# Attention, two gated layers: a longer written order, other denominators, other column groups in PV

## The chip, the cores and the metric

The kernel runs on one core of a Trainium2 chip. The metric is the device time of one execution in microseconds; the kernel before took 491.09 us (median of 3 runs, 490.27 to 493.12). Names used below: PE is TensorE, the matrix engine; DVE is VectorE; ACT is ScalarE; POOL is GpSimd; SP is SyncE, whose queue issues the transfers.

## The reference, cut to what matters

```
# mLSTM: 2 batches x 8 heads, 768 positions, 40 per head
m_new = max(f + m, i);  f_s = exp(f + m - m_new);  i_s = exp(i - m_new)
C = f_s * C + i_s * outer(v, k);   n = f_s * n + i_s * k
denom = max(|n . q|, 1);           y = sigmoid(o_gate) * (C q) / denom
# layer 1 on 1536 rows of 320, inner width 1536
x = (sigmoid(x @ w_gate) * (x @ w_val)) @ w_out
# layer 2: the same widths, rows normalised first, silu gate
xn = x / rms(x) * g;  x = (silu(xn @ w_gate) * (xn @ w_val)) @ w_out
```

## The kernel before

**Tiles and stages.** The 768 positions are cut into 6 chunks of 128 (c) and the 2 batches (b). For each chunk and batch the attention is computed in four quarters (q, four heads each): a scan turns the gates into weights between positions (F), S is k against q, P the product of the two, PV the product of P with v, I the part that comes from the state C, U and UC the new state. H then adds PV and I, multiplies by the output gate and divides by the denominator. The result x is transposed on PE (XP, L492 and L493) and split into a high and a low float32r part (XH, XL). Layer 1 takes chunks 0 to 3 one by one and 4 and 5 as a pair (name p), layer 2 takes the chunks in three pairs, the first called q. Each layer has 12 tiles of weights (f, 0 to b in hexadecimal): T is the up-projection (eight matmuls with the gate half, eight with the value half: L549 for one chunk, L596 for a pair), S and M the activation and the products, H the split, Y the down-projection (L577, L574, L627).

**Weights.** A packed weight tile is loaded (LW, LZ; line 179), its top half is unpacked into one of two scratch tiles `tops` (WT, ZT; L192 on ACT, L194 on DVE), DVE combines it with the mantissa (WM, WO, ZM; L199), and ACT, DVE and POOL split it further. Layer 2's raw tiles and the low half of layer 2's transposed input share one tag, `wraw`, with two buffers; `new_xT2` takes the high and the low half's buffers together.

**PV.** From chunk PB = 2 on, P and v are split into three bf16 parts each, and a head takes three accumulating matmuls of 126, 84 and 42 columns into three column groups (L416), which H adds in three additions a quarter (L226). Chunks 0 and 1 use float32 directly (L418).

**Denominators.** `abs_1` makes max(|nq|, 1) with two DVE instructions (L441, L442), a reciprocal follows (L461, L475), and a product with x broadcast over the head (L226; three of chunk 0's four quarters on POOL).

**What sets the order.** PLAN is a written list of step names; the steps are issued in that order and pinned, so each engine and SP's queue execute their shares in it. It goes up to layer 2's steps q0 and q1 (NP = 2), after which the remaining steps of layer 2 are issued in a loop and placed by the scheduler. PE opens with 13 idle matmuls (WARM, L869), and six steps D (`m_idle`, L555) issue two idle matmuls each.

Of the kernel before, what the change touches and what calls it, by code (L numbers as in the profile page):

```python
# [7 lines left out]
F32 = mybir.dt.float32  # L8
F32R = mybir.dt.float32r
# [28 lines left out]
PB = 2  # L38
# [3 lines left out]
N32 = (4,2)  # L42
# [7 lines left out]
K00 H01b WO0 WM0 F02 PV00 H00a Lqk01 S01 WG0 F03 P03 Lgr D0 Lmr Ltok01 Rf1 Ri1 LW1 LW2 Rf2 WLG0 H00b V01 WLH0 WOH0 XR00 Rie Rfe U00 Rer P02 K02 Rz PV03  # L50
D1 PV02 K03 Lfd Lqg10 Lsel Lqk10 Lf10 O01 WR0 WLR0 WLS0 U01 WT1 XP00 H03a WM1 Lf11 H02a WO1 H03b UC00 Ltok10 Lqg11 LW3 H02b Rt1 D2 Rt2 WT2 UC01 Lf13
LW4 Lqk11 Lf12 XR01 WR1 WO2 WM2 XP01 D3 WLR1 XH00 XL00 D4 D5 XH01 XL01 Rel UM00 WR2 Rc1 F11 Rg F10 WG2 WG1 Rgc Rc2 T00 S10 WLG1 WLS1 TS00 WOH2 WLS2
WLH1 TH00 P10 P11 Y000 Y001 I10 WT3 K11 V10 T01 PV11 PV10 IH10 WLR2 WO3 WM3 WLG2 K10 WG3 WLH3 WLG3 TS01 WR3 TH01 WT4 T02 TS02 H10a WLS3 Ltok11 WLR3 F12
F13 S11 Y011 TH02 P13 P12 UM01 V11 T03 I11 Y010 PV13 Y021 PV12 WO4 WM4 TS03 O10 H10b WR4 O11 WG4 LW6 LW9 Lqk20 LW5 Ltok20 WLR4 H10c IH11 U10 WLS4 WLH4
# [960 lines left out]
```

## Time and profile before

| | |
|---|---|
| median of 3 runs | 491.09 us |
| the profiled execution | 491.04 us |
| its span, first to last instruction | 489.3 us |
| PE busy | 472.6 us (97%) |
| DVE busy | 277.6 us (57%) |
| ACT busy | 208.6 us (43%) |
| POOL busy | 207.2 us (42%) |
| mean granted clock of PE | 0.978 |

Times in the trace count from the first instruction. Matmuls overlap, so the difference between starts says more of their rate than the mean of one, and a float32 matmul is recorded as two. The granted clock is 1.00 at 2.4 GHz and half of that at 1.2 GHz.

### The profile page before, as it was taken

Reading aid. Unit: us, or ns where it says so; the run is one execution under the profiler, and the core shown is the slowest. Engines: PE = TensorE matmul, PEld = TensorE weight load, DVE = VectorE, ACT = ScalarE, POOL = GpSimd, SP = SyncE. Lnnn points to the kernel's source line nnn. Section 1 sums busy time; section 2 is a strip of 40 time slices with the busy share of each in tenths; the row PEclk is TensorE's granted clock in tenths of the full one; section 3 lists DMA queues with packets and bytes.
Section 4 is the critical chain, followed back from the end, with each engine's and each line's share of the span. In section 5 each row is a group of like instructions: output and inputs, shape, how many; then the busy total and the mean of one; then the engine's idle time right before and its main releaser. Section 6 shows DMA issues by size and latency. Waiting matters only on the chain.

```text
span 489.3 us, 8000 instructions
## 1 busy us (share of the span) xinstructions
PE 472.6 (97%) x3074; PEld 421.7 (86%) x3074; DVE 277.6 (57%) x518; ACT 208.6 (43%) x459; POOL 207.2 (42%) x252
## 2 busy tenths in 40 slices
PE   8999999998999999999999997999999999999997
PEld 5888899998998999978888886888888888888886
DVE  6789668896799998947366655222342222332223
ACT  4655686544534435632657654222332222322222
POOL 3555577556575546222466763322222221323221
PEclk9589999999999999999999998999999999999999
DMA  6699901143051431334433220000010000100001
GB/s 220 244 333 380 373 32 58 43 140 101 15 141 58 144 110 57 125 107 161 162 109 132 82 81 1 0 1 0 1 54 1 1 1 0 55 0 1 1 1 54
DMA packets 13277, 43.80 MB, mean 90 GB/s; under 512 B 1623, under 2 KB 5095, under 8 KB 13239
## 3 DMA queue, kind: packets, MB, share of 16 engines
q1 hardware_dynamic: 13094, 43.16, 26.1%
q8 instruction: 24, 0.39, 0.3%
q10 hardware_dynamic: 144, 0.14, 0.1%
q14 instruction: 15, 0.11, 0.1%
HBM read 41.24 MB, written 2.05 MB: 88 GB/s over the span
## 4 chain that ended last, share of the span: by engine, by line
PE 71%; DVE 17%; DMA 4%; ACT 3%; issue 2%; POOL 1%; SPq 1%; ACTq 0%; DVEq 0%; POOLq 0%
PE g L596 18%; PE a L596 18%; PE o L627 17%; PE g L549 8%; PE o L577 4%; DVE hs L226 3%; DVE ft L229 3%; DMA early<-fd 2%; DVE x L226 2%; DVE p L226 1%; DMA fb<-fd 1%; DVE sig L226 1%; PE o L869 1%; PE o L549 1%; DVE p L130 1%
## 5 line engine op out<-in xcount | busy, mean ns | idle before, releaser
L130 POOL TENSOR_TENSOR ft<-p,fb 128x512 fp32r<-128x512 f32 x47 | 61.4, 1307 | 164.0 <-ACT fb L232 156.7
L549 PE MATMUL g<-xT,w 128*128 128x256 f32 x640 | 82.6, 283 | 0.4 <-DVE sig L226 0.4
L226 DVE TENSOR_TENSOR p<-p,g 128x512 f32<-128x512 f32 x36 | 24.8, 688 | 101.8 <-ACT p L600 101.8
L549 PEld LDWEIGHTS g<-xT,w 128*128 128x128 f32 x640 | 78.0, 188 | 1.4 <-DVE sig L226 0.7
L627 PE MATMUL o<-w,fb 128*128 128x320 f32 x384 | 73.5, 310 | 0.0
L596 PE MATMUL g<-xT,w 128*128 128x512 f32 x240 | 67.8, 398 | 3.6 <-DVE p L226 3.6
L627 PEld LDWEIGHTS o<-w,fb 128*128 128x128 f32 x384 | 62.2, 188 | 4.2
L596 PE MATMUL a<-xT,w 128*128 128x512 f32 x240 | 64.7, 398 | 0.0
L232 ACT ACTIVATE fb<-p 128x512 fp32r<-128x512 f32 (+1 forms) x49 | 30.4, 622 | 77.1 <-DVE p L226 58.4
L600 ACT ACTIVATE p<-g 128x512 f32<-128x512 f32 x48 | 28.5, 595 | 74.1 <-PE g L596 69.5
L226 DVE TENSOR_TENSOR p<-p,a 128x512 f32<-128x512 f32 (+1 forms) x49 | 33.0, 675 | 39.4 <-PE a L596 24.3
L596 PEld LDWEIGHTS g<-xT,w 128*128 128x128 f32 x240 | 43.4, 189 | 11.5 <-DVE p L226 4.1
L596 PEld LDWEIGHTS a<-xT,w 128*128 128x128 f32 x240 | 44.9, 190 | 9.3
L130 POOL TENSOR_TENSOR h<-sig,h 128x256 fp32r<-128x256 f32 x42 | 35.1, 838 | 39.4 <-ACT h L232 37.6
L577 PE MATMUL o<-w,h 128*128 128x320 f32 x252 | 46.5, 319 | 0.0
L627 PE MATMUL o<-w,ft 128*128 128x320 f32 x192 | 45.8, 310 | 0.0
L577 PEld LDWEIGHTS o<-w,h 128*128 128x128 f32 x252 | 37.8, 189 | 1.1
L627 PEld LDWEIGHTS o<-w,ft 128*128 128x128 f32 x192 | 32.7, 188 | 0.4
L130 POOL TENSOR_TENSOR w<-wc,w 128x256 fp32r<-128x256 f32 (+2 forms) x37 | 24.9, 677 | 18.8 <-ACT w L232 9.7
L596 PE MATMUL g<-wraw,w 128*128 128x512 f32 x108 | 31.6, 400 | 0.0
L596 PE MATMUL a<-wraw,w 128*128 128x512 f32 x108 | 31.1, 393 | 0.0
L232 ACT ACTIVATE h<-sig 128x256 fp32r<-128x256 f32 x42 | 17.3, 414 | 25.3 <-DVE sig L226 15.5
(168 smaller groups left out, 747.6 us busy)
## 6 DMA issues: line engine op xcount, KB each, us to landing
wraw<-in_w_dram SPq DMA_DIRECT2D x24, 959.8 KB, 9.0
tok<-in_tok_dram SPq DMA_DIRECT2D x10, 488.0 KB
fb<-fd SPq DMA_DIRECT2D x18, 256.0 KB, 3.3
raw<-in_qk_dram SPq DMA_DIRECT2D x24, 160.0 KB
out_dram<-xn SPq DMA_DIRECT2D x12, 160.0 KB, 1.8
qg<-in_qg_dram SPq DMA_DIRECT2D x8, 180.0 KB, 4.9
early<-in_tok_dram SPq DMA_DIRECT2D x2, 488.0 KB
early<-fd SPq DMA_DIRECT2D x2, 256.0 KB
```

The costliest lines, as they stand in the source:

```text
L130: eng.tensor_tensor(out=out, in0=a, in1=b, op=ALU.subtract)
L226: eng.tensor_tensor(out=out, in0=a, in1=b, op=op)
L229: v.tensor_tensor_scan(out=out, data0=a, data1=b, initial=initial, op0=op0, op1=op1)
L232: a_.activation(out=out, in_=x, func=AF.Copy, scale=scale)
L549: nc.tensor.matmul(out=g[:, m, :], lhsT=w[:, m, ws, :], rhs=x[xs // 3][:, xs % 3, :], start=(i == 0), stop=(i == 7))
L577: nc.tensor.matmul(out=o, lhsT=h[:, hs, b * L:(b + 1) * L], rhs=wo_t[f][:, ws, :], start=(n == 1 and i == 0), stop=(n == NF and i == 2))
L596: nc.tensor.matmul(out=g, lhsT=w[:, m, ws, :], rhs=x[xs // 3][:, xs % 3, :], start=(i == 0), stop=(i == 7))
L600: a_.activation(out=s, in_=keep["w", k, f, 0], func=AF.Sigmoid)
L627: nc.tensor.matmul(out=o_ps[key][:, 0:DM], lhsT=h[hs][:, n], rhs=wo_t[f][:, ws, :], start=(c == 1 and i == 0), stop=(c == NF and i == 2))
L869: nc.tensor.matmul(out=t, lhsT=warm[:, 0:128], rhs=warm, start=True, stop=True)
```

## The change

The program's numbers change: PB from 2 to 3, NP from 2 to 5, ND from 6 to 24, and PLAN is written anew in full. Of the code, `abs_1` goes: the absolute value is an activation on ACT, the reciprocal a step of its own (H..r), and the minimum with 1 is taken in the last product, which is on DVE throughout. From chunk 3 on a head of PV takes four matmuls into two column groups (84, 42, 84, 42 columns), and H adds two groups a quarter; chunk 2 uses float32 PV. `tops` are handed out from a list of free ones. `new_xT2` takes the low half's buffer when the low half is written. Each D issues one idle matmul.

```diff
-PB = 2
+PB = 3
-NP = 2
+NP = 5
-ND = 6
+ND = 24
 PLAN = """
-Lga Gm Gf1 Gf2 Gfe Gid Gmz Gse Gi1 Gms Lgs Ltok00 Gfh Gie Gt Gfl Fb01 Fb00 Rm Lqk00 S00 F01 P01 LW0 Fb02 O00 Gtg V00 Fb03 Lms PV01 F00 H01a K01 P00 WT0
+D0 D1 D2 Lga Gm Lsel D3 D4 D5 D6 D7 D8 Gse Gms Gid Lgr Lgs Lqg10 Gf1 Lqk01 Lqk00 Rm Gf2 Gfe Gi1 Gmz Gfh Gfl Lms Fb01 Ltok01 Lmr Ltok00 Gie Gt D9 D10
...
-        up = tops[turn["t"] % 2]
-        turn["t"] += 1
+        up = free.pop(0)
...
+        left[f] = left.get(f, WC) - (n.stop - n.start)
+        if left[f] == 0:
+            left.pop(f)
+            free.append(up)
...
-                for k in range(3):
-                    n = (3 - k) * E
-                    nc.tensor.matmul(out=ps[:, 3 * i * E:3 * i * E + n], lhsT=p[:, k, i, :], rhs=w[:, 0:n], start=(k == 0), stop=(k == 2))
+                for n, (k, s0, ns, d) in enumerate(((0, 0, 2, 0), (0, 2, 1, 1), (1, 0, 2, 0), (2, 0, 1, 0))):
+                    at = (2 * i + d) * E
+                    nc.tensor.matmul(out=ps[:, at:at + ns * E], lhsT=p[:, k, i, :], rhs=w[:, s0 * E:(s0 + ns) * E], start=(n == 0), stop=(n == 3))
...
-    def abs_1(r, nq):
-        v.tensor_scalar(out=r, in0=nq, scalar1=1.0, scalar2=None, op0=ALU.max)
-        v.scalar_tensor_tensor(out=r, in0=nq, scalar=-1.0, in1=r, op0=ALU.mult, op1=ALU.max)
+    def h_abs(key, nq):
+        r = out_t[key] = p2.tile([128, 8, 1], F32, tag="r", name="r")[:, 0:nq.shape[1]]
+        a_.activation(out=r, in_=nq, func=AF.Abs)
+    def h_r(key):
+        v.reciprocal(out=out_t[key], in_=out_t[key])
+    def h_mul(eng, key, x):
+        r = out_t.pop(key)
+        eng.scalar_tensor_tensor(out=x, in0=r.to_broadcast([128, r.shape[1], D]), scalar=1.0, in1=x, op0=ALU.min, op1=ALU.mult)
...
-                pv = pv_t.pop((c, 2 * b + q))[:, 0:12 * E].rearrange("p (h s e) -> p h s e", h=4, s=3)
-                for k in range(3):
+                pv = pv_t.pop((c, 2 * b + q))[:, 0:8 * E].rearrange("p (h s e) -> p h s e", h=4, s=2)
+                for k in range(2):
                     tt(v, hs[:, 4 * q:4 * q + 4], pv[:, :, k], hs[:, 4 * q:4 * q + 4], ALU.add)
...
-    def new_xT2(pair):
-        if (2, pair) not in xT:
+    def new_xT2(pair, part):
+        t = xT.setdefault((2, pair), [])
+        if part == len(t):
...
-        for _ in range(2):
-            nc.tensor.matmul(out=g, lhsT=warm[:, 0:128], rhs=warm, start=True, stop=True)
+        nc.tensor.matmul(out=g, lhsT=warm[:, 0:128], rhs=warm, start=True, stop=True)
```

On DVE, around layer 2's first steps, before: the raw tile of weight 9 (`raw_3688`) and the two products (`p_3679`, by the gate half in g and the value half in a) of step q1.

```order
L199 SCALAR_TENSOR_TENSOR tok_3666<-wraw_3577,top0_82 128x960
L130 TENSOR_TENSOR w_3651<-wc_3401,w_3651 64x128
L130 TENSOR_TENSOR w_3676<-tok_3666,w_3676 128x320
L130 TENSOR_TENSOR w_3651<-wc_3401,w_3651 128x320
L199 SCALAR_TENSOR_TENSOR raw_3688<-wraw_3657,top1_83 128x960
L130 TENSOR_TENSOR w_3690<-raw_3688,w_3690 64x128
L226 TENSOR_TENSOR p_3679<-p_3679,g_3618 128x512
L226 TENSOR_TENSOR p_3679<-p_3679,a_3627 128x512
```

The same place now, where the last weight tile (b, `wraw_3658`) is unpacked:

```order
L660 SCALAR_TENSOR_TENSOR xn_3569<-o3_2967,ss_3694,rmsg_76 128x320
L231 TENSOR_TENSOR p_3709<-p_3709,g_3676 128x512
L231 TENSOR_TENSOR p_3709<-p_3709,a_3604 128x512
L231 TENSOR_TENSOR p_3738<-p_3738,g_3613 128x512
L195 CAST top1_83<-wraw_3658 128x960
L200 SCALAR_TENSOR_TENSOR wc_3742<-wraw_3658,top1_83 128x960
L231 TENSOR_TENSOR p_3738<-p_3738,a_3719 128x512
L131 TENSOR_TENSOR w_3510<-wc_3424,w_3510 128x320
```

Before, the products of step q1 stand behind the raw tile of weight 9; now those of q0 to q3 and the first of q4 (`p_3738`) stand ahead of the last weight.

On DVE, chunk 2, batch 1, the end of its attention before (hs is the sum of PV and I, r the denominator, x the result):

```order
L226 TENSOR_TENSOR hs<-a,hs 128x168 x6
L226 TENSOR_TENSOR x<-x,hs 128x320
L441 TENSOR_SCALAR r<-hs 128x8
L442 SCALAR_TENSOR_TENSOR r<-hs,r 128x8
L461 RECIPROCAL r<-r 128x8
L226 TENSOR_TENSOR x<-x,r 128x320 x2
```

And now:

```order
L131 TENSOR_TENSOR w<-wc,w 128x2x256
L231 TENSOR_TENSOR x<-x,hs 128x320
L453 RECIPROCAL r<-r 128x8
L231 TENSOR_TENSOR sig<-sig,g 128x256
L457 SCALAR_TENSOR_TENSOR x<-r,x 128x320
```

The addition to hs is now one instruction of 128x336, which stands 19 rows earlier, and other work stands between the parts of the chain.

On SP, at the start, before: the loads of broadcast gates for chunk 1 (out of `fd`, steps Lf10, Lf11, Lf13 and Lf12 in this order) and the weights (`wraw`, steps LW3 and LW4).

```order
L170 DMA fb_313<-fd_94 128x512
L151 DMA early_285<-in_tok_dram 128x976
L159 DMA early_327<-in_qg_dram 120x384
L179 DMA wraw_329<-in_w1_dram 128x3839
L170 DMA fb_342<-fd_94 128x512
L179 DMA wraw_344<-in_w1_dram 128x3839
L137 DMA raw_346<-in_qk_dram 40x1024 x2
L170 DMA early_327<-fd_94 128x512
```

And now (Lf10, Lf11, LW2, Lqk11, Lf12, Lf13, LW3, LW4):

```order
L171 DMA early_138<-fd_94 128x512
L171 DMA fb_326<-fd_94 128x512
L181 DMA wraw_345<-in_w1_dram 128x3839
L138 DMA raw_405<-in_qk_dram 40x1024 x2
L171 DMA early_307<-fd_94 128x512
L171 DMA fb_491<-fd_94 128x512
L181 DMA wraw_493<-in_w1_dram 128x3839
L181 DMA wraw_498<-in_w1_dram 128x3839
```

All four gate loads of chunk 1 now stand ahead of weights 3 and 4, and weight 2 stands behind the first two of them.

## Rows read from the trace of the kernel before

**Rows 1.** The page: span, and busy time of PE.

```profile
span 489.3 us, 8000 instructions
PE 472.6 (97%) x3074; PEld 421.7 (86%) x3074; DVE 277.6 (57%) x518; ACT 208.6 (43%) x459; POOL 207.2 (42%) x252
```

**Rows 2.** Stretches: start:end length, busy by engine, granted clock, DMA share, GB/s.

```profile
100.00:120.00 20.00, 18.20 (x168) 17.31 (x167) 17.61 (x40) 9.30 (x25) 10.62 (x15) 1.00 0.41 121
...
280.00:300.00 20.00, 16.38 (x76) 13.65 (x75) 12.41 (x26) 10.84 (x28) 10.60 (x16) 0.94 0.14 50
...
380.00:400.00 20.00, 20.00 (x104) 17.38 (x102) 5.50 (x8) 4.86 (x8) 3.88 (x3) 1.00 0.00 1
```

**Rows 3.** What PE waited for: us in total, times, longest.

```profile
PE g L596 <- DVE p L226: 3.6, 1, 3.6
PE a L492 <- DVE x L226: 1.7, 1, 1.7
...
PE a L492 <- DVE C L433: 1.2, 1, 1.2
PE o L492 <- DVE xT L130: 0.9, 1, 0.9
PE o L492 <- DVE x L226: 0.9, 1, 0.9
```

**Rows 4.** The chain that ended last, 286 to 314 us: start, us, what.

```profile
288.31 4.51 DMA wraw<-in_w_dram
...
292.85 1.28 ACT top L192
...
294.15 1.17 DVE raw L199
...
295.99 0.70 DVE p L226
...
296.73 3.16 PE g L596 x8
299.89 2.38 PE a L596 x8
...
311.22 1.85 PE g L596 x8
```

**Rows 5.** DVE in order of time, 106 to 112.5 us, chunk 2.

```profile
106.97 2.03 DVE L226 TENSOR_TENSOR hs<-a,hs 128x168 f32<-128x168 f32 x6
...
109.47 0.84 DVE L441 TENSOR_SCALAR r<-hs 128x8 f32<-128x8 f32 x1
110.35 0.78 DVE L442 SCALAR_TENSOR_TENSOR r<-hs,r 128x8 f32<-128x8 f32 x1
...
111.28 1.55 DVE L226 TENSOR_TENSOR x<-x,r 128x320 f32<-128x320 f32 x2
```

**Rows 6.** Two stretches of PV: float32 (16 records), bf16 (24), PE alone.

```profile
35.47:37.17 1.70, 1.70 (x16) 1.00 1.06 269
134.28:135.24 0.96, 0.95 (x24) 1.00 0.00 0
```

**Rows 7.** The same chain, 0 to 60 us.

```profile
1.30 5.73 PE o L869 x13
...
22.30 5.83 DMA fb<-fd
28.14 10.57 DMA early<-fd
38.81 3.60 DVE ft L229 x2
```

**Rows 8.** The page's DMA issues: count, size, us to landing (median).

```profile
fb<-fd SPq DMA_DIRECT2D x18, 256.0 KB, 3.3
```

**Rows 9.** ACT in order of time, 15 to 19 us: one of four table loads.

```profile
15.52 1.28 ACT L239 ACT_TABLE_LOAD   x1
```

**Rows 10.** What SP's queue waited for: us in total, times, longest.

```profile
SPq L170 <- DVE ft L229: 26.1, 4, 19.4
```

More of the change, by code (lines that the diff above doesn't have):

```diff
@@ L51 @@
[L51 to L54, printed above, removed]
@@ L174, in mlstm_moe_kernel @@
     wg_t, wo_t, wraw, wc, conv, o32 = {}, {}, {}, {}, {}, {}
+    free, left = list(tops), {}
     def load_w(src, f):
@@ L455, in a_h2, with hs0, x0 @@
     def a_h2(c, b):
-        hs = hs_t.pop((c, b))
         x = x_t[c][:, b]
-        r = p2.tile([128, 8, 1], F32, tag="r", name="r")
-        tt(v, x, x, hs[:, :, 0:D], ALU.mult)
-        abs_1(r, hs[:, :, D:D + 1])
-        v.reciprocal(out=r, in_=r)
-        out_t[c, b] = r
-    def a_h3(c, b, eng=None):
-        x = x_t[c][:, b]
-        tt(eng or v, x, x, out_t.pop((c, b)).to_broadcast([128, 8, D]), ALU.mult)
-    def h_0(qd):
-        b, o = qd // 2, 4 * (qd % 2)
-        hs = pv_t.pop((0, qd))[:, o * E:(o + 4) * E].rearrange("p (h e) -> p h e", h=4)
-        x = x_t[0][:, b, o:o + 4]
-        r = out_t[0, qd] = p2.tile([128, 8, 1], F32, tag="r", name="r")[:, 0:4]
-        abs_1(r, hs[:, :, D:D + 1])
-        tt(v, x, x, hs[:, :, 0:D], ALU.mult)
-        v.reciprocal(out=r, in_=r)
-    def h_1(qd, eng):
-        b, o = qd // 2, 4 * (qd % 2)
-        x = x_t[0][:, b, o:o + 4]
-        tt(eng, x, x, out_t.pop((0, qd)).to_broadcast([128, 4, D]), ALU.mult)
+        tt(v, x, x, hs_t[c, b][:, :, 0:D], ALU.mult)
+    def hs0(qd):
+        o = 4 * (qd % 2)
+        return pv_t[0, qd][:, o * E:(o + 4) * E].rearrange("p (h e) -> p h e", h=4)
+    def x0(qd):
+        return x_t[0][:, qd // 2, 4 * (qd % 2):4 * (qd % 2) + 4]
+    def h_0(qd):
+        x = x0(qd)
+        tt(v, x, x, hs0(qd)[:, :, 0:D], ALU.mult)
     def x_r(key, x):
@@ L521, in rows @@
         return x_t[c][:, b].rearrange("p h d -> p (h d)")
-    def new_xT2(pair):
-        if (2, pair) not in xT:
-            hi = p2.tile([128, 6, T], F32R, tag="xT", name="xT").rearrange("p s t -> p (s t)")
-            lo = p2.tile([128, WC], I64, tag="wraw", name="wraw").bitcast(F32R)[:, 0:6 * T]
-            xT[2, pair] = [t.rearrange("p (s t) -> p s t", s=3) for t in (hi, lo)]
-        return xT[2, pair]
+    def new_xT2(pair, part):
+        t = xT.setdefault((2, pair), [])
+        if part == len(t):
+            if part == 0:
+                t.append(p2.tile([128, 6, T], F32R, tag="xT", name="xT").rearrange("p s t -> p (s t)"))
+            else:
+                t.append(p2.tile([128, WC], I64, tag="wraw", name="wraw").bitcast(F32R)[:, 0:6 * T])
+            t[part] = t[part].rearrange("p (s t) -> p s t", s=3)
+        return t
     def to_xT2w(pair, i, k):
-        t = new_xT2(pair)
-        x_all((2, k), xn[k], t, i, "g")
+        new_xT2(pair, 0)
+        x_all((2, k), xn[k], new_xT2(pair, 1), i, "g")
     ORD = ((0, 0), (3, 0), (1, 1), (4, 1), (2, 2), (0, 3), (1, 4), (2, 5))
@@ L776, in mlstm_moe_kernel @@
                 for q in qs:
+                    op(f"A0{q}", lambda q: h_abs((0, q), hs0(q)[:, :, D:D + 1]), q)
                     op(f"H0{q}a", h_0, q)
-                    op(f"H0{q}b", h_1, q, (g_, g_, g_, v)[q])
+                    op(f"H0{q}r", h_r, (0, q))
+                    op(f"H0{q}b", lambda q: h_mul(v, (0, q), x0(q)), q)
             else:
@@ L854, in mlstm_moe_kernel @@
         op(f"RP{k}", lambda k: x_p((2, k), xn[k], "a"), k)
-        op(f"RH{k}", x_h, (2, k), lambda: new_xT2(0), k)
-        op(f"RL{k}", x_l, (2, k), lambda: new_xT2(0), k)
+        op(f"RH{k}", x_h, (2, k), lambda: new_xT2(0, 0), k)
+        op(f"RL{k}", x_l, (2, k), lambda: new_xT2(0, 1), k)
     body = nc.cur_bb.bb.instructions
```

83 lines of the change are left out of this document (45 added, 38 removed).

## The prediction

> **What bounds the kernel now.** I read the page's head first, then stretches of the span, then what the matrix engine (PE) waited for, then the chain of work that ended last, and only then single stretches of VectorE (DVE). PE is busy for 472.6 of 489.3 us [rows 1], so its work sets most of the time. Busy does not mean useful, though: the stretch 380 to 400 us is full at a granted clock of 1.00 with every other engine near a quarter, while 280 to 300 us holds 16.38 busy us of 20 at 0.94, and 100 to 120 us holds 18.20 with DVE at 17.61 [rows 2]. So there are three regimes. Layer 2 after about 305 us is pure PE work, and nothing in the change touches it. While attention runs, as in 100 to 120 us, DVE is nearly full, and PE pauses where DVE is late. At the very start the chain runs over transfers.
>
> The pauses with a name are few [rows 3]: one of 3.6 us before L596 (the up-projection of layer 2), and four of 1.7, 1.2, 0.9 and 0.9 us before L492, the transposes of x that follow the attention of a chunk. Together 8.3 us.
>
> **The 3.6 us pause and what follows it.** The chain shows it link by link [rows 4]: a weight transfer of 4.51 us from 288.31, ScalarE's unpacking of it for 1.28, DVE's L199 for 1.17, and only then, at 295.99, the product p that PE waits for. DVE executes in order, and the L199 of that weight stood ahead of the product. PE resumes at 296.73 at the lower of its two clock levels: eight matmuls take 3.16 us and the next eight 2.38, against 1.85 at 311.22. So the loss is 3.62 + (3.16 - 1.85) + (2.38 - 1.85) = 5.5 us.
>
> The new order writes out five steps of layer 2's second part instead of two (NP). In DVE's row the products of steps 0 to 3 and one of step 4 now stand ahead of the last weight's L199 (L200 there), where before the first product of step 1 stood behind a late L199. The low half of the transposed input takes its raw-weight buffer later than the high half (new_xT2 is split in two), but four weight loads (5, 8, 7, b) then still share the one buffer that is left, where three did before (8, 9, a): the gain is in the order, not in the buffers. PE thus has four steps of work, about 4 x 2 x 1.85 = 15 us by the row at 311.22, to cover a transfer of 4.51 plus 1.28 + 1.17 us of unpacking. I take back 4.9 of the 5.5 us; the bounds are 0 and 5.5. What is late next there is the rival below.
>
> **Denominators and PV, on DVE.** In the chunk 2 chain [rows 5] six additions take 2.03 us, then L441 0.84 and L442 0.78 us, then the products. L441 and L442 vanish in all 14 places (4 in chunk 0, 10 later); each is replaced by one Abs on ScalarE, which runs beside the product x with h, and the minimum rides in the last product at the price of that product. The Abs adds a hop to ScalarE and back, which the product of x with h, or other work of DVE in between, hides. The six additions become four in chunks 3 to 5 and one of double width in chunk 2, which saves at least 2 x 2.03/6 = 0.7 us of each such chain. The chain in front of a transpose therefore shrinks by 0.7 (additions) + 0.3 to 1.6 (L441, L442: 0.84 + 0.78 is the slow case) us, against pauses of 0.9 to 1.7. The multiplication that GpSimd made in three of chunk 0's four quarters comes to DVE, costing at most 0.8 us each (the last of [rows 5] holds two products of double width in 1.55) and sparing a hop. Chunk 2 also drops 8 subtractions on DVE, 12 copies on ScalarE and 4 subtractions on GpSimd. Of the 4.7 us of pauses before L492 I take half, **2.2 us**; the bounds are 0 (the new order spends the slack elsewhere: in the rows of the order the parts of a chain now stand apart, with other work between) and 4.7.
>
> **PV, on PE.** Chunk 2 goes from three bf16 matmuls a head to one float32 matmul, recorded as two. [rows 6]: 16 such records, eight heads, took 1.70 us, so 0.21 us a head; 24 bf16 records, eight heads, took 0.96, so 0.12 a head. Sixteen heads cost 16 x (0.21 - 0.12) = **+1.5 us**. For chunks 3 to 5 a head goes from three matmuls (126 + 84 + 42 columns) to four (84 + 42 + 84 + 42), again 252 columns but one more weight load: between 0.12 (by columns) and 4 x 0.96/24 = 0.16 us (by count). Over 48 heads that is 0 to 1.9; with no row that separates them I take the middle, **+1.0 us**. Nothing hides these, since PE is the bound.
>
> The Trainium skill, page "FP8 and Floating Point Precision", section "TensorE Precision Notes", says that true FP32 takes four passes through the array. By that alone float32 PV would need 4 x 42 = 168 columns a head against 252 in bf16 and would be cheaper, an estimate of two thirds of 0.12 us; the row disagrees (0.21 against 0.12 us), and by the rule the sum below would be lower by about 2.1 us.
>
> **The start.** The chain there is transfers and DVE [rows 7]: the first gate broadcast lands 5.83 us after its issue at 22.30, the one issued at 28.14 takes 10.57, and two scans follow, 3.60 us. The median of these 18 loads is 3.3 us [rows 8]; the 10.57 is a queue full of weights, since two weight loads stand ahead of it on SP. In the new order it stands ahead of them, and one weight load fewer precedes the first broadcast. This leg can shrink by 10.57 - 5.83 = 4.7 us or more. Two of ScalarE's four table loads, 1.28 us each [rows 9], go as well, because both exponentials of the rows stand ahead of the first sigmoid. Against it: nine idle matmuls now stand on PE ahead of the first broadcast of the gates; at 5.73/13 = 0.44 us each [rows 7] that is up to 4.0 us, in which the scan Rm, now ahead of the gates on DVE, and GpSimd's work run anyway. Idle matmuls in all go from 6 x 2 to 24, so 12 more, 5.3 us at 0.44; I cost the rest of them at nothing, since they stand where PE waits for gates and for x, and at up to 1.3 us where that cover is gone. And weights 3 and 4 now stand on SP behind a gate load that waits for a DVE scan; SP spent 26.1 us in such waits before [rows 10]. So what is late next is the weights, and I take only half of the leg: **-2.4 us**, with bounds of -6 and +4.
>
> **The sum**, against the profiled execution's own 491.04 us (span 489.3 and 1.7 around it; the median of the runs, 491.09, is the same): 491.04 - 4.9 - 2.2 + 1.5 + 1.0 - 2.4 = **484.0 us**. The rest of the reordered stretch, 60 to 280 us, I take as neither better nor worse, give or take 3.
>
> **Rivals.** (a) *The late weight only moves.* The low half of the input (RL2) now stands on DVE right behind the cast of weight 7, a load with a single buffer, and PE's first step of layer 2's second part needs RL2. If that load ends 4 us after PE arrives, the pause returns at the new place, half clock included, and the 4.9 us are not won: 484.0 + 4.9 = 488.9 us. For it: loads of 4.51 us in a chain of one buffer. Against it: between the L200 of weight 8, which frees that buffer, and the point where RL2 is needed, PE has two half steps (1.85 us each by [rows 4]), eight output tiles and a transpose. 20%.
> (b) *The start is slower, and the kernel with it.* If the nine idle matmuls push the gate broadcasts, DVE's scan of the second gate load ends late, and as SP holds weights 3 and 4 behind it, PE runs out of weights for tile 3. It decides from about 5 us of delay at that scan: then 4 us of idle matmuls, 5 us of PE waiting and some 1.8 us at the lower clock replace my -2.4, and 484.0 + 2.4 + 10.8 = 497 at the full price, 494 if half of the wait finds other work. Against it: PE's new row has chunk 1's attention to do there. 13%.
> (c) *The relief is larger.* The pauses before L492 vanish whole (-2.5 more) and the start's leg comes in full (-2.3 more): 479.2 us. For it: 24 fewer additions at 2.03/6 = 0.34 us are 8 us of DVE alone, in a stretch where it is nearly full [rows 2]. 14%.
> That the change does not do what it says can be left aside: the order shows every removed and added instruction.
>
> **How the numbers follow.** The forecast, 484.0, has 53%, with its own range of 481 to 488. With (a), (b), (c) at 20, 13 and 14%, a range of 478 to 492 leaves out (b) and little else. A measurement of this kernel can tell about 0.5% from no change, 2.5 us. Faster by more than that means below 488.6: the forecast, (c) and somewhat under half of (a), less a little for the forecast's upper edge: 0.69. Slower means above 493.5: (b), 0.13. The rest, 0.18, is no change.
>
> **What would show it.** In the profile after: no pause of PE before the up-projection of layer 2 and a granted clock of 1.00 from 60 us on (step 1); pauses before the transposes under 2.5 us in sum (step 2); chunk 2's 32 float32 records 0.1 us apart, and eight heads of bf16 PV in 1.0 to 1.3 us (step 3); gate broadcasts of chunk 1 landing within 6 us, and the fourth weight tile's matmuls without a pause before 45 us (step 4). It would be wrong if PE's pauses in 60 to 280 us grew, which no row of before can rule out, since all of that order is new.

## The result, and the profile after

The changed kernel took **479.22 us** (median of 4 runs, 478.22 to 480.58) against 491.08 us for the kernel before on the same chip: ratio 0.9754, 95% interval 0.9715 to 0.9793. That is faster by 11.9 us: inside the range of 478 to 492, but 4.8 us below the forecast of 484.0 and outside the 481 to 488 that the forecast had for itself. The profiled execution took 479.62 us with a span of 477.8 us.

The page of the changed kernel, the head and the share of the chain of waits by engine:

```profile
span 477.8 us, 7976 instructions
PE 467.4 (98%) x3116; PEld 422.4 (88%) x3118; DVE 261.2 (55%) x463; ACT 201.3 (42%) x459; POOL 200.1 (42%) x245
PEclk9969999999999999999999999999999999999999
...
PE 94%; DMA 3%; issue 1%; POOL 1%; DVE 0%; SPq 0%; ACT 0%; DVEq 0%
```

DVE lost 16.4 us of work against [rows 1], and the chain that ended last lies on PE for 94% of the span. What PE waited for, in us in total, times, longest:

```profile
PE a L399 <- issue: 3.1, 1, 3.1
PE g L424 <- DVE ft L234: 1.3, 1, 1.3
PE o L878 <- POOL gates L869: 1.3, 1, 1.3
PE g L318 <- DVE fs L131: 0.5, 1, 0.5
...
PE o L496 <- ACT rem L237: 0.2, 1, 0.2
```

Against [rows 3] the pauses before the transposes (L492 there, L495 here) and before layer 2's up-projection (L596 there, L601 here) are gone; of the transposes one of 0.2 us is left, before L496 at 21 us. A new pause of 3.1 us has come, at 25 us. The stretches say the same, first of the kernel before, then of the changed one (columns as in [rows 2]):

```profile
60.00:280.00 220.00, 215.02 (x1675) 200.00 (x1674) 167.19 (x317) 114.39 (x271) 122.72 (x152) 1.00 0.31 100
280.00:320.00 40.00, 36.38 (x178) 31.14 (x177) 17.36 (x33) 15.63 (x35) 15.77 (x20) 0.96 0.07 25
```

```profile
60.00:280.00 220.00, 219.96 (x1727) 207.39 (x1726) 149.92 (x271) 114.03 (x278) 117.72 (x147) 1.00 0.34 110
280.00:320.00 40.00, 40.00 (x210) 35.30 (x209) 21.79 (x35) 14.65 (x31) 20.30 (x23) 1.00 0.00 1
```

PE stood 4.98 us idle in 60 to 280 us before and 0.04 us after; in 280 to 320 us it was 3.62 and is 0.

**A ledger by stage.** Idle time alone misses matmuls that merely follow one another more slowly. So I gave every useful matmul in the trace the spacing that its shape has when nothing is waited for (for example 118 ns for 128x256 and 231 ns for 128x512, float32; 27 to 54 ns for bf16 PV), added these up, and read the lag: the time on the clock less the work begun by then. The growth of the lag in a stretch is what that stretch loses. The stages and the work add up to the span. The level of a stage hangs on the spacings that are taken (with average spacings for the small float32 shapes the middle stage is 12.9 us before and 5.7 after, instead of 14.2 and 6.8); differences between kernels hang on them by up to some 0.5 us.

| kernel | useful PE work | lost 0 to 60 | 60 to 280 | 280 to 320 | 320 to end | span |
|---|---|---|---|---|---|---|
| before | 439.6 | 25.3 | 14.2 | 5.6 | 4.6 | 489.3 |
| changed | 441.6 | 26.1 | 6.8 | -0.2 | 3.6 | 477.8 |
| difference | +2.0 | +0.8 | -7.4 | -5.8 | -1.0 | -11.5 |

(The differences add up to -11.4; the rest is rounding.) A second profile of the changed kernel, below, has 27.1 and 7.6 in the first two stages, so about 1 us of either is what executions differ by.

### The profile page after: what moved, and what is told of

Its sections match the earlier page's. It is cut to its first block, busy times and chain, and to the rows that moved or that the text cites. A ratio compares the mean times of both kernels' runs of the same rounds, so it can differ in the third digit from the quotient of the medians.

```text
span 477.8 us, 7976 instructions
## 1 busy us (share of the span) xinstructions
PE 467.4 (98%) x3116; PEld 422.4 (88%) x3118; DVE 261.2 (55%) x463; ACT 201.3 (42%) x459; POOL 200.1 (42%) x245
## 3 DMA queue, kind: packets, MB, share of 16 engines
q1 hardware_dynamic: 13094, 43.16, 27.1%
## 4 chain that ended last, share of the span: by engine, by line
PE 94%; DMA 3%; issue 1%; POOL 1%; DVE 0%; SPq 0%; ACT 0%; DVEq 0%
PE g L601 19%; PE a L601 18%; PE o L632 18%; PE g L555 17%; PE o L582 8%; PE o L555 3%; PE a L332 2%; PE a L424 2%; PE o L579 1%; PE a L422 1%; PE a L399 1%; PE o L399 1%; DMA early<-in_qg_dram 1%; DMA tok<-in_tok_dram 1%; DMA gates<-in_gate_s_dram 1%
## 5 line engine op out<-in xcount | busy, mean ns | idle before, releaser
L555 PE MATMUL g<-xT,w 128*128 128x256 f32 x640 | 85.6, 289 | 0.0
L555 PEld LDWEIGHTS g<-xT,w 128*128 128x128 f32 x640 | 81.0, 195 | 1.0
L632 PE MATMUL o<-w,fb 128*128 128x320 f32 x384 | 74.8, 311 | 0.0
L601 PE MATMUL g<-xT,w 128*128 128x512 f32 x240 | 66.5, 393 | 0.0
L601 PE MATMUL a<-xT,w 128*128 128x512 f32 x240 | 63.1, 392 | 0.0
L131 POOL TENSOR_TENSOR h<-sig,h 128x256 fp32r<-128x256 f32 x42 | 36.5, 877 | 38.8 <-ACT h L237 36.6
L601 PEld LDWEIGHTS a<-xT,w 128*128 128x128 f32 x240 | 44.3, 188 | 8.5
L231 DVE TENSOR_TENSOR p<-p,a 128x512 f32<-128x512 f32 (+1 forms) x49 | 32.9, 676 | 30.7 <-PE a L601 23.8
L601 PEld LDWEIGHTS g<-xT,w 128*128 128x128 f32 x240 | 43.3, 188 | 7.2 <-ACT xT L237 0.5
L632 PE MATMUL o<-w,ft 128*128 128x320 f32 x192 | 46.9, 310 | 0.0
L131 POOL TENSOR_TENSOR w<-wc,w 128x256 fp32r<-128x256 f32 (+2 forms) x37 | 24.4, 663 | 21.0 <-ACT w L237 17.0
L601 PE MATMUL a<-wraw,w 128*128 128x512 f32 x108 | 30.8, 390 | 0.0
L601 PE MATMUL g<-wraw,w 128*128 128x512 f32 x108 | 30.8, 391 | 0.0
L564 ACT ACTIVATE sig<-g 128x256 f32<-128x256 f32 x40 | 15.1, 379 | 29.6 <-PE g L555 19.5
```

Source lines behind the costliest of these rows:

```text
L131: eng.tensor_tensor(out=out, in0=a, in1=b, op=ALU.subtract)
L231: eng.tensor_tensor(out=out, in0=a, in1=b, op=op)
L555: nc.tensor.matmul(out=g[:, m, :], lhsT=w[:, m, ws, :], rhs=x[xs // 3][:, xs % 3, :], start=(i == 0), stop=(i == 7))
L564: a_.activation(out=s, in_=keep["g", c, f][:, 0, :], func=AF.Sigmoid)
L601: nc.tensor.matmul(out=g, lhsT=w[:, m, ws, :], rhs=x[xs // 3][:, xs % 3, :], start=(i == 0), stop=(i == 7))
L632: nc.tensor.matmul(out=o_ps[key][:, 0:DM], lhsT=h[hs][:, n], rhs=wo_t[f][:, ws, :], start=(c == 1 and i == 0), stop=(c == NF and i == 2))
```

## The experiments

Every run has the kernel before beside it, and ratios are to that; its medians were 488.96 to 489.16 us there, so ratios compare better than microseconds. I began with two theories of the 7.4 us between 60 and 280 us: A, they are relief of DVE; B, they come from the order.

**The old order with all the new operations.** The steps A, H..r stand in the old list where the old denominators stood.

```diff
-NP = 5
+NP = 2
 PLAN = """
-D0 D1 D2 Lga Gm Lsel D3 D4 D5 D6 D7 D8 Gse Gms Gid Lgr Lgs Lqg10 Gf1 Lqk01 Lqk00 Rm Gf2 Gfe Gi1 Gmz Gfh Gfl Lms Fb01 Ltok01 Lmr Ltok00 Gie Gt D9 D10
+Lga Gm Gf1 Gf2 Gfe Gid Gmz Gse Gi1 Gms Lgs Ltok00 Gfh Gie Gt Gfl Fb01 Fb00 Rm Lqk00 S00 F01 P01 LW0 Fb02 O00 Gtg V00 Fb03 Lms PV01 F00 A01 H01a H01r
...
```

> The written order of the kernel before (with its two steps into layer 2), and all the new operations: ScalarE's absolute value, the minimum within the product, two column groups, float32 in chunk 2. Theory A (the 7.5 us that came off between 60 and 280 us are relief of VectorE): most of it shows here too, 5 to 7 us, less about 2 us of added matmul time, so 486 to 488 against 491; the pause ahead of layer 2's up-projection, about 5 us, stays. Rival B (they come from the order alone): 490 to 493, the added matmul time is all that is seen.

Measured: 482.38 us (482.22 to 482.88), ratio 0.9876 (0.9838 to 0.9914); ledger: work 441.6, lost 22.2, 6.6, 5.6, 4.6. The middle lost as little as in the changed kernel, in the old order: theory A. The pause ahead of layer 2 stayed. More than I expected was won, because the start gained 3.1 us as well.

**Chunk 2 in three bf16 parts again, old order.** From the run above:

```diff
-PB = 3
+PB = 2
```

> As the run with the old order, but with chunk 2 in three bfloat16 parts again, as in the kernel before: only the denominators and the column groups of chunks 3 to 5 are new. Theory A1 (the splits of chunk 2 held the path in the old order): 3 to 5 us slower than the run with all new operations, so 490 to 492. A2 (the denominators held it): 1 to 2 us faster than that run, since the float32 matmuls' added time is gone, so 485 to 487. Under rival B: 490 to 491.5.

Measured: 481.4 us (480.46 to 483.58), ratio 0.9861 (0.9816 to 0.9906); ledger: work 440.2, lost 24.4, 6.6, 3.7, 4.8. A2, though some 4 us below the level that was expected, like the run that it is taken from: leaving out chunk 2's 24 copies and subtractions bought nothing in the middle (6.6 either way), and its float32 matmuls cost 441.6 - 440.2 = 1.4 us of PE.

**Only the denominators, old order.** Three column groups and three additions again as well.

```diff
-                for n, (k, s0, ns, d) in enumerate(((0, 0, 2, 0), (0, 2, 1, 1), (1, 0, 2, 0), (2, 0, 1, 0))):
...
+                for k in range(3):
+                    n = (3 - k) * E
...
-                for k in range(2):
+                for k in range(3):
```

> The order and the matmuls of the kernel before (three bfloat16 parts in chunk 2, three column groups); only the denominators are new: ScalarE's absolute value, the minimum within the product, and chunk 0's last product on VectorE for all four quarters. If the denominators alone free the old order's middle: as fast as the run that has the column groups too (481.4) or up to 1 us slower, 0.984 to 0.988 of the kernel before. If the smaller additions of chunks 3 to 5 are what counts: 487 to 490, 0.995 to 1.002.

Measured: 482.26 us (481.87 to 483.91), ratio 0.9861 (0.9835 to 0.9887); ledger: work 439.6, lost 23.8, 8.5, 5.5, 4.7. So the denominators alone take 5.7 of the middle's 14.2 us. The column groups with their smaller additions take 1.9 more there, not far above the 1 us by which executions differ, and add 0.6 us of work over 64 heads (chunk 2 has them here too).

**The same, with chunk 0 as before.** Is it the short chains of the later chunks, or the product that left GpSimd in chunk 0 and moved the start?

```diff
-                    op(f"A0{q}", lambda q: h_abs((0, q), hs0(q)[:, :, D:D + 1]), q)
...
-                    op(f"H0{q}b", lambda q: h_mul(v, (0, q), x0(q)), q)
+                    op(f"H0{q}b", h_1, q, (g_, g_, g_, v)[q])
```

> The run with the old order and only the denominators new, but chunk 0 as in the kernel before (two VectorE instructions, the last product of three quarters on GpSimd): only chunks 1 to 5 have ScalarE's absolute value and the minimum within the product. If the middle (60 to 280 us) is freed by the short chains of chunks 1 to 4 there: the pauses ahead of the transpositions stay away, 482 to 485, 0.985 to 0.991 of the kernel before. If it is freed because chunk 0 leaves GpSimd and the stream past 60 us starts at another point: the pauses come back, 488 to 491, 0.997 to 1.003.

Measured: 482.59 us (481.25 to 483.68), ratio 0.9873 (0.9839 to 0.9907); ledger: work 439.6, lost 22.6, 8.7, 5.4, 4.7. The middle is relieved just as well, so it is the chains of chunks 1 to 5. What PE waited for in 60 to 280 us in this run, in full:

```profile
PE g L552 <- DVE sig L227: 0.4, 1, 0.4
PE a L328 <- issue: 0.4, 1, 0.4
PE o L495 <- DVE x L450: 0.3, 1, 0.3
```

Of the pauses of [rows 3] that lay in this stretch (1.7, 0.9 and 0.9 us) one of 0.3 us is left. What was taken off DVE, in groups of the kernel before by line, count, busy and mean ns:

```profile
L441 DVE TENSOR_SCALAR r<-hs 128x8 f32<-128x8 f32 x10 | 4.0, 401 | 0.0
L442 DVE SCALAR_TENSOR_TENSOR r<-hs,r 128x8 f32<-128x8 f32 x10 | 3.7, 366 | 0.3
```

About 0.77 us in each of ten chains, in a row and ahead of the transposes, were enough in the old order. That mean has two prices in it. Of the 20 instructions 11 took 0.16 to 0.17 us; the other nine, 0.38 to 0.84 us, began while a TENSOR_TENSOR of GpSimd was running and ended 0.02 to 0.03 us after it, in all nine cases. One undisturbed instruction, and what ran beside the two slow ones of [rows 5]:

```profile
101.82 0.16 DVE L441 TENSOR_SCALAR r<-hs 128x8 f32<-128x8 f32 x1
```

```profile
109.16 1.95 POOL L130 TENSOR_TENSOR w<-o,w 128x320 fp32r<-128x320 f32 x2
111.06 0.75 POOL L226 TENSOR_TENSOR vv<-tok,tg 128x336 f32<-128x336 f32 x1
```

```profile
111.16 0.20 DVE L461 RECIPROCAL r<-r 128x8 f32<-128x8 f32 x1
```

The two of GpSimd's L130 end at 110.29 and 111.11 us, L441 and L442 at 110.31 and 111.13; the reciprocal took its 0.20 us while GpSimd's next instruction ran. At 0.16 to 0.17 us each the 20 would take 3.3 us instead of 7.7, so more than half of what the change took off these chains was waiting for GpSimd. No run here moves GpSimd's work alone.

**The new order with the old denominators and column groups.** Chunk 2 stays in float32: the new order leaves its parts no turn in the buffers that they share with the weights, so that combination wasn't tried.

```diff
-        a_.activation(out=r, in_=nq, func=AF.Abs)
+        v.tensor_scalar(out=r, in0=nq, scalar1=1.0, scalar2=None, op0=ALU.max)
+        v.scalar_tensor_tensor(out=r, in0=nq, scalar=-1.0, in1=r, op0=ALU.mult, op1=ALU.max)
...
-                for k in range(2):
+                for k in range(3):
```

> The changed kernel's order, chunk 2 in float32 as there, but the old denominators (absolute value and maximum by two VectorE instructions, plain product) and three column groups with three additions. Theory A (relief of VectorE): 3 to 5 us of the middle are lost again, 482 to 484 against 479. Rival B (the order alone): within 0.5 us of 479, since VectorE is busy 55% of the time and TensorE runs ahead of nothing.

Measured: 482.47 us (482.29 to 482.81), ratio 0.9875 (0.9830 to 0.9921); ledger: work 441.1, lost 28.1, 8.3, -0.1, 3.6. About the time that A gave, but not by its reason: the middle lost only 1.5 us more than in the changed kernel, and 2.0 us went at the start. So theory B holds too, in part. In this order the two instructions no longer stand directly in front of their reciprocal: in chunk 2, batch 1, they start at 100.03 and 100.49 us and the reciprocal at 111.16, where the old order has 0.03 us between them in all ten chains. How much is the order by itself is not shown, since this run also lacks chunk 2's splits, and the old order with the old denominators and without those splits was not run. The two are not a sum: the denominators in the old order take the middle from 14.2 to 8.5, the new order with float32 in chunk 2 takes it to 8.3, and everything together to 6.8.

**Only the absolute value back on DVE, new order.**

> The changed kernel with the absolute value by two VectorE instructions (with the maximum), as in the kernel before, instead of ScalarE's one; the minimum stays in the product, where it then changes nothing. If the denominators' place on VectorE is what holds TensorE in any order: 3 to 5 us slower than 479. If only the old order was sensitive to it: within 1 us of 479, with VectorE busy some 2 to 4 us longer and no pause of TensorE over 1 us between 60 and 280 us.

The edit is the first of the two above, without the plain product. Measured: 481.57 us (480.87 to 481.89), ratio 0.9842 (0.9819 to 0.9866); ledger of its fastest execution: lost 27.1, 7.1, -0.2, 3.5. The middle did not react, though DVE was busy 268.0 us instead of 261.2. By the times it is some 2 us slower than the changed kernel, less than the first theory and more than the second wanted; but it ran on another chip than the changed kernel, and by ratio its interval touches that of the changed kernel's second set of runs below (0.9767 to 0.9824). What the trace shows of it lies before 60 us, where executions differ anyway. That part stays open.

**Two steps into layer 2 instead of five, new order.**

```diff
-NP = 5
+NP = 2
...
-ZOL6 N412 ZLS9 N502 ZLG8 Mq21 Mq22 Tq01 ZLR9 N413 Ypb0 Ypb3 Tq31 Tq40 Ypa3 Mq01 Mq02 N503 ZO7 Hq21 Hq01 ZGa N400 ZLG5 ZLG7 Hq22 ZLH7 Hq02 ZLH6 Tq10 Sq1
+ZOL6 N412 ZLS9 N502 ZLG8 Tq01 ZLR9 N413 Ypb0 Ypb3 Ypa3 Mq01 Mq02 N503 ZO7 Hq01 ZGa N400 ZLG5 ZLG7 ZLH7 Hq02 ZLH6 Tq10 Sq1 Mq11 ZLGa LZb N401 N402 Tq11
...
```

> The changed kernel with the written order reaching two steps into layer 2 instead of five; the rest of the order and all operations as there. Theory (the pause ahead of layer 2's up-projection goes because more steps of the order can be placed before it): the pause comes back with 3 to 5.5 us, 482 to 485 against 479. Rival (the pause goes because VectorE comes earlier to the expert layer's chain, whatever the order reaches): within 1 us of 479, no pause over 1 us near 290 us.

Measured: 484.37 us (483.65 to 485.11), ratio 0.9898 (0.9875 to 0.9920); ledger: lost 26.1, 7.1, 4.3, 3.6. Its stretch, its waits and the pieces of its chain of waits after the pause:

```profile
280.00:300.00 20.00, 17.59 (x79) 14.83 (x78) 14.69 (x24) 8.58 (x21) 12.39 (x16) 0.91 0.00 1
```

```profile
PE o L632 <- DVE ss L652: 2.1, 1, 2.1
```

```profile
289.01 2.37 PE g L601 x8
291.38 1.84 PE a L601 x8
```

A pause is back, 2.1 us of standing still and then eight matmuls that take 2.37 us against 1.84, at a mean granted clock of 0.91 in the stretch. Here PE waits for the norm of x, not for the product behind the late weight of [rows 4]. That weight is no longer late: SP's last weight load, issued at 288.31 us before, is issued some 17 us earlier in the changed kernel (4.6 us of it are the lead that the kernel has by then) and, the second line, in this run:

```profile
271.11 0.33 SPq L181 DMA_DIRECT2D wraw<-in_w_dram  x1
```

```profile
270.91 0.33 SPq L181 DMA_DIRECT2D wraw<-in_w_dram  x1
```

So two things went with the new order: the late weight, by an earlier load, whatever the reach; and a wait for the norm, which is there with two steps and not with five. The loss with two steps is 4.3 us against 5.6 before and none with five. I read the second gain as the three further steps' work standing in front of what is late.

**The start: idle matmuls.** In the changed kernel PE stood from 24.95 to 28.05 us and then ran slowly. Four pieces of its chain of waits, and the stretch after:

```profile
24.95 3.10 issue
28.05 1.54 PE a L399 x6
...
34.22 3.56 PE g L555 x16
...
39.02 2.12 PE g L555 x16
```

```profile
30.00:40.00 10.00, 10.00 (x60) 9.65 (x61) 8.02 (x16) 4.31 (x9) 2.45 (x4) 0.60 1.02 418
```

The interaction I11 (L399) needs a bank of PSUM that the product P11 must leave first: its first weight load waits for DVE from 24.23 to 27.99 us, and P11, the first of the two in the last line, ends at 27.95. DVE's part of that, in order of time:

```profile
24.10 1.23 DVE L234 TENSOR_TENSOR_SCAN ft<-early,ident 128x512 f32<-128x512 f32 x1 [0.32 <-DMA early<-fd]
25.93 1.23 DVE L234 TENSOR_TENSOR_SCAN ft<-fb,ident 128x512 f32<-128x512 f32 x1 [0.60 <-DMA fb<-fd]
27.25 1.29 DVE L231 TENSOR_TENSOR p<-a,ft 128x512 f32<-128x512 f32 x2
```

The first run puts 14 idle matmuls in front of I11:

```diff
-V10 K11 WLH1 D23 XP00 I11 PV11 Lqk11 Lf12 XL01 IH11 WG0 WLS0 WLS1 O10 I10 PV10 XH00 XL00 WT2 WO2 WLR1 WM2 IH10 WOH2 WR2 H10a WLR2 WLR0 T01 K10 WLH0
+V10 K11 WLH1 D23 XP00 D24 D25 D26 D27 D28 D29 D30 D31 D32 D33 D34 D35 D36 D37 I11 PV11 Lqk11 Lf12 XL01 IH11 WG0 WLS0 WLS1 O10 I10 PV10 XH00 XL00 WT2
```

> The changed kernel with 14 more idle matmuls ahead of the interaction I11, where TensorE stands for 3.1 us at 25 us and then runs at the half clock until about 38 us. If the half clock costs path time there (10 us of work at half speed that would be some 3 us shorter): 476 to 478. Rival: the stretch up to 40 us ends with the gate loads and VectorE whatever the clock is, and the result is 479 to 480; third, the matmuls, if TensorE isn't idle long enough for them, delay it by up to 3 us: 480 to 482.

Measured: 479.7 us (476.66 to 481.68), ratio 0.9814 (0.9758 to 0.9871). The median lies in the rival's range, but no case holds for all four executions: they took 476.66, 478.62, 480.78 and 481.68 us, in the order of their mean granted clocks, 0.999, 0.992, 0.986 and 0.982. The profile, which is of the fastest, has 24.1, 5.8, -0.2 and 3.7 us lost. I read this as: filling this pause helps where the clock doesn't fall elsewhere, which the next run puts to the test.

The second run fills the smaller pauses too, 12 more idle matmuls between 13 and 23 us:

```diff
-UM00 Lf10 Lf11 H01a H01r H00r H00b H01b Rt1 D17 Rg Rgc XP01 Rt2 LW2 Rc1 Rc2 XR00 XH01 WOH1 WR0 WR1 D18 D19 D20 D21 D22 S10 UM01 F10 F11 P11 P10 WLG1
...
+Lqk10 WO0 WM0 A01 XR01 WG1 D23 D24 UM00 Lf10 Lf11 H01a H01r H00r H00b H01b D25 D26 Rt1 D27 D28 D29 Rg Rgc XP01 Rt2 LW2 Rc1 Rc2 XR00 XH01 WOH1 WR0 WR1
...
```

> The changed kernel with 26 more idle matmuls: the 14 ahead of I11, and 12 more in the pauses that the run with the 14 showed at 13.5, 18.6 and 20.5 to 22.5 us. If in its slower executions (478.6 to 481.7 at mean clocks of 0.992 to 0.982, against 476.7 at 0.999) the clock fell in these pauses: 475 to 478 with a mean clock of 0.99 or more in most executions. Rival: the clock falls all the same in some executions, or the added matmuls push the start by 1 to 2 us: 478 to 481, no better than the changed kernel.

Beside it, on the same chip, the changed kernel itself:

> The changed kernel once more, beside the runs with filled pauses and on the same chip: 478 to 481, 0.971 to 0.980 of the kernel before, and mean clocks of 0.984 to 0.989 as in its first four executions; a wider spread would show that the stretch at the half clock moves here too.

Measured: **477.1 us** (475.42 to 477.48, 6 runs), ratio 0.9757 (0.9730 to 0.9784), with the fills; 479.01 us (477.77 to 481.53, 6 runs), ratio 0.9795 (0.9767 to 0.9824), without. All six runs with the fills are below all six without, and their mean granted clocks are 0.999 or 1.000, against 0.984 to 0.989. This version beats both kernels, by 1.9 us over the changed one. The stretches of the run with the fills, and of the second profile of the changed kernel:

```profile
10.00:20.00 10.00, 10.00 (x99) 8.92 (x98) 9.28 (x16) 5.42 (x16) 6.84 (x15) 1.00 0.91 342
20.00:30.00 10.00, 10.00 (x72) 6.59 (x72) 8.77 (x18) 6.79 (x18) 4.80 (x8) 1.00 0.88 261
30.00:40.00 10.00, 9.89 (x83) 9.13 (x83) 9.49 (x17) 5.65 (x12) 3.32 (x5) 1.00 1.02 415
```

```profile
10.00:20.00 10.00, 6.93 (x60) 6.20 (x58) 7.25 (x10) 3.97 (x6) 4.91 (x11) 0.82 0.83 308
20.00:30.00 10.00, 10.00 (x45) 8.71 (x45) 5.58 (x17) 4.38 (x18) 3.59 (x6) 0.50 0.79 240
30.00:40.00 10.00, 9.39 (x88) 8.37 (x87) 9.61 (x15) 7.22 (x17) 5.79 (x9) 1.00 1.03 395
```

```profile
PE g L424 <- DVE p L231: 3.1, 1, 3.1
```

In this second profile the half clock came at about 16.5 to 30 us instead of 28 to 38, after a pause of 3.1 us in front of chunk 0's PV (L424, the last line) instead of I11: same kernel, another place. With the fills the first 60 us lose 22.9 us instead of 26.1 or 27.1; but that profile is of the fastest of its six executions, and the second one of the changed kernel of its slowest (481.53 us), so the medians are the fairer price. Nor does the mean clock order the times everywhere: among the six without the fills the fastest, 477.77 us, has 0.985 and the slowest 0.986.

**Without the idle matmuls at the front**, the first nine of the changed kernel's 24:

```diff
-D0 D1 D2 Lga Gm Lsel D3 D4 D5 D6 D7 D8 Gse Gms Gid Lgr Lgs Lqg10 Gf1 Lqk01 Lqk00 Rm Gf2 Gfe Gi1 Gmz Gfh Gfl Lms Fb01 Ltok01 Lmr Ltok00 Gie Gt D9 D10
+Lga Gm Lsel Gse Gms Gid Lgr Lgs Lqg10 Gf1 Lqk01 Lqk00 Rm Gf2 Gfe Gi1 Gmz Gfh Gfl Lms Fb01 Ltok01 Lmr Ltok00 Gie Gt D0 D1 Fb02 Fb03 D2 D3 Gtg F01 F02
```

> The changed kernel without the first nine idle matmuls, that is without 18 of the matmuls that run ahead of its first loads' use. If they only warm the clock before any useful work can start: within 1 us of the changed kernel, since TensorE waits for the loads there anyway. If the clock at 10 to 20 us hangs on them: the half clock comes there as in the kernel before (0.54 in that stretch), and 2 to 4 us slower. If they delay the first useful matmuls: up to 1 us faster.

(The expectation's "18 of the matmuls" is a slip: each of the nine steps issues one.) Measured: 480.63 us (480.50 to 481.40), ratio 0.9837 (0.9806 to 0.9869), with a granted clock of 0.50 in 10 to 20 us and 0.52 in 20 to 30 us. The clock of the second case, at less than its price: 1.6 us slower than the changed kernel beside it, and one of that kernel's six executions (481.53 us) was slower than all four of these.

**The old order's start, then the new order.** Up to step T02 the list of the first experiment, from there the changed kernel's.

```diff
-D0 D1 D2 Lga Gm Lsel D3 D4 D5 D6 D7 D8 Gse Gms Gid Lgr Lgs Lqg10 Gf1 Lqk01 Lqk00 Rm Gf2 Gfe Gi1 Gmz Gfh Gfl Lms Fb01 Ltok01 Lmr Ltok00 Gie Gt D9 D10
+Lga Gm Gf1 Gf2 Gfe Gid Gmz Gse Gi1 Gms Lgs Ltok00 Gfh Gie Gt Gfl Fb01 Fb00 Rm Lqk00 S00 F01 P01 LW0 Fb02 O00 Gtg V00 Fb03 Lms PV01 F00 A01 H01a H01r
...
```

> All new operations; the written order of the kernel before as far as the third transposition group of layer 1 (about the first 55 us), and from there the changed kernel's order with its five steps into layer 2. If start and rest are independent: the start of the run with the old order (3 to 4 us ahead of the changed kernel at 60 us) and the changed kernel's rest without a pause, so 475 to 477. Rival: the work that the new start had done early (loads, parts of weights) is missing later, and the gain is given back by 140 us: 479 to 481.

Measured: 480.44 us (479.54 to 483.09), ratio 0.9826 (0.9789 to 0.9863); ledger: lost 28.2, 5.1, 0.1, 4.6. The time is the rival's, its reason is not: the lead never came about, since at 60 us it was already behind both orders, with the granted clock at 0.63 and 0.69 in 10 to 30 us and again at 0.66 in 40 to 50 us. The middle gave nothing back. Why the joint costs this was not settled.

## Why the prediction was right or wrong

The direction and the range held; the forecast was off by 4.8 us. Against its terms, by the ledger, 60 to 280 us gave 5.2 us more, layer 2 0.9 more, the end 1.0 that was not forecast, and PV cost 0.5 less, while the start came out 3.2 us worse. The start's miss hid part of the middle's: that the total came closer than these two terms is luck.

**Layer 2's up-projection, -4.9.** Measured -5.8 in the ledger. The pause went as forecast: PE was busy 40.00 of 40 us, clock 1.00, and taking the reach back to two steps brought a loss of 4.3 us back. The reason was half right: I had thought that four steps of PE's work would cover the late weight. The weight is not late at all now, its load is issued some 17 us earlier, with either reach; what the further steps cover is the wait for the norm. Rival (a) did not come about: no pause anywhere in 280 to 320 us.

**Denominators and PV on DVE, -2.2, and the rest of 60 to 280 us, 0.** Measured -7.4. This is the term that was mis-sized, and it is the first half of the mechanism of rival (c). That (c)'s time, 479.2, is what came out is chance: its two parts were -2.5 and -2.3 beyond the forecast, and measured -5.2 and +3.2. I took half of the pauses with a name; those in this stretch all vanished, and all but 0.3 us with the denominators alone and the old order. Two of the four were misread: the one of 1.2 us lay at 51.9 us, in the start, and waits for the state C, and one of 0.9 us waits for the split of a transposed x; neither is a wait for a denominator. And the price of 0.84 and 0.78 us that I called the slow case has a reason in the trace, GpSimd's instruction beside it, which I did not look for. And the stretch held more loss than its named pauses: 14.2 us, of which only 4.98 were idle. The remainder, matmuls that follow one another more slowly, shrank by some 2.5 us with it; what slowed them single record by record was not followed up. Of the parts, in the old order, the denominators carry 5.7 us, the column groups 1.9, and with these in place chunk 2's splits nothing to be seen. The new order with float32 in chunk 2 takes most of it without either; what it would take alone was not run. In the changed kernel one addition of double width stands in chunk 2 for the six of 2.03 us in [rows 5], here with the product that holds the minimum, of the other batch:

```profile
93.08 0.51 DVE L231 TENSOR_TENSOR hs<-a,hs 128x336 f32<-128x336 f32 x1
...
94.15 0.66 DVE L457 SCALAR_TENSOR_TENSOR x<-r,x 128x320 f32<-128x320 f32 x1
```

**PV on PE, +1.5 and +1.0.** Measured +1.4 (the run with chunk 2 in parts against the one without) and +0.6 (two column groups against three, over 64 heads), both in the ledger's work, +2.0 together. The stretch of eight heads of bf16 PV in the changed kernel, 32 of its records, and of four float32 heads, against [rows 6]:

```profile
142.89:143.93 1.04, 1.04 (x36) 1.04 (x34) 1.04 (x5) 0.00 (x0) 0.15 (x1) 1.00 0.65 134
```

```profile
86.28:87.10 0.82, 0.82 (x11) 0.82 (x9) 0.79 (x3) 0.81 (x3) 0.39 (x2) 1.00 0.07 20
```

1.04 us for eight heads against 0.96 is near the end of my bracket that goes by columns, not its middle. The float32 heads stand 0.2 us apart, as in the row that I had used. The Trainium skill, page "FP8 and Floating Point Precision", section "TensorE Precision Notes", says four passes for true FP32; the estimate from it in the prediction, that float32 would be cheaper, is not borne out by these runs either.

**The start, -2.4.** Measured +0.8 (and +1.8 in the second profile): the wrong sign, within its bounds. What I named as signs came true and still did not make the term: the gate load for chunk 1, issued at 20.73 us, was scanned from 24.10 on, two of four table loads went, the fourth weight tile ran without a pause. The step that failed is the one from a shorter leg to a shorter start. I followed the transfers, and did not ask which bank the first matmuls of chunk 1 need: I11 stood next in PE's row, waiting for P11, and PE paid 3.1 us and then ten at the lower clock. In the second profile the 3.1 us stood elsewhere, before chunk 0's PV, and I11 waited 0.6 us, so I11 is one place of the loss and not its only one. The fills show the price of such pauses: 3 to 4 us of the start's loss by the profiles, 1.9 us between the medians. Rival (b) had the kind of loss right, PE standing and then slow, but not its place and not its 10.8 us.

**Not predicted:** the end, 320 us on, loses 1.0 us less in the new order than in the old one (3.5 to 3.7 against 4.6 to 4.8 in all runs but the one with the joint). I have not looked into it.

## What to carry to other kernels

A few small instructions in a row on an engine that is half busy can hold the bound engine for far more than the pauses that bear their name (here 5.7 us against at most 3.5): measure the loss of a stage against its undisturbed work, not by its idle time, and look at single durations, not only at the mean, for what holds them. Two cures of the same stall need not add up (14.2 us to 8.5, 8.3 and, together, 6.8), so try each alone before pricing both. Where a step is moved forward, check what its PSUM bank waits for as carefully as its inputs, and try idle matmuls in the pauses of the start (here 1.9 us).

## What was not expected of the hardware

The stretch at the lower of the two clock levels (granted 0.5, 1.2 GHz) has no fixed place at the start: in two profiles of the same kernel it lay at 28 to 38 and at about 16.5 to 30 us, from about the end of a pause of PE of 3.1 us in both. With the pauses filled six executions lay within 2.1 us at 0.999 to 1.000; with one of them filled four executions spread over 5.0 us, and their times fell in the order of their clocks (0.999 to 0.982). A pause doesn't always bring it: ahead of layer 2, in the old order, 3.5 us of standing still came with a granted clock of 1.00 and a loss of 3.7 us in the stretch from 280 to 320 us in one run, and with 0.96 and 5.5 us in another. And DVE's two instructions on 128x8 numbers, 0.40 and 0.37 us on average in the kernel before, took 0.16 to 0.17 us undisturbed, less than the 0.20 us of the reciprocal on the same tile; beside a TENSOR_TENSOR of GpSimd they ended 0.02 to 0.03 us after that instruction, up to 0.84 us after their start, while the reciprocal kept its 0.20.
